# Attention followed by a gated MLP on one core: queries of pairs two to eight held in another order, and one bias row picked sooner

## The chip, the cores and the metric

The kernel runs on one core of a Trainium2 chip. The metric is the device time of one execution in microseconds (us), the median of several executions. Before the change it is 356.12 us (three runs, 356.06 to 356.26). The engines are named as in the profile: PE is TensorE (matmul), PEld its weight load, DVE VectorE, ACT ScalarE, POOL GpSimd, SP SyncE, which here only issues transfers.

## What is computed

There are 8 batches of 8 heads, 576 positions, head size 64. With q, k, v of shape (8, 8, 576, 64) and a gate s of shape (8, 8, 576):

```python
scores = (q @ k.T) / sqrt(64)
cum = cumsum(maximum(s, 0.0), axis=-1)
bias = -(cum[:, :, :, None] - cum[:, :, None, :])
scores = where(causal, -1e9, scores + minimum(bias, 0.0))
attn = softmax(scores)
x = (attn @ v) with the 8 heads of a position side by side   # (4608, 512)
h = x @ w_in                                                # (4608, 2048)
out = (h * clip(h + 3, 0, 6) / 6) @ w_out                   # (4608, 512)
```

Since cum only grows, the minimum changes nothing below the diagonal, and the bias is a difference of two numbers, one for the query and one for the key. The order of the queries within a head is free as long as bias, mask and output follow it: each query's row is computed by itself. The order of the keys is not touched by this change.

## The kernel before

**Pairs and rounds.** The 64 heads go in 32 pairs (two heads of one batch, four pairs to a batch, `PPB`). The main loop has one round per pair `p`. A round computes the scores of pair p (transposed: keys on partitions, queries along the free dimension), their exponentials into `P`, and the products with v (`av`), and prepares the queries and keys of pair p + 1. From round 4 on, pieces of the MLP (`m1`: x @ w_in with the gate, `m2`: the product with w_out) are set between the pieces of attention by `group()`, in the order of a list written out by hand (`plan`). So the order of each engine's instructions is fixed when the kernel is built.

**Queries and keys.** Pairs 0 to 10 (`NPE` = 11) come from DRAM as f16 tokens `tok` on 96 partitions (`load_qk`, line 116; GpSimd issues the transfer): each partition holds six successive positions of a head. TensorE transposes them, six transposes per operand, into a PSUM tile `pt` (`transpose_in`, line 242). A transpose takes two positions side by side, so positions of one parity come out on partitions 0 to 63 and the others on 64 to 127. Two copies (`transpose_out`, line 259; `head_out`, line 273, for one head) then bring each half down to partitions 0 to 63 of `qk`, and put the positions in order: a copy reads three columns with a stride of 96 and writes with a step of two elements. Both query copies are VectorE's; of the key copies, the first half is ScalarE's and the second VectorE's. Later pairs are transposed by the DMA's crossbar (line 286).

**Bias.** `cum` is split in parts and held in `rows_of`, tile row 1 for keys and tile row 0 for queries. For pairs 1 and up the rows are carried by a transfer (`load_aug`, line 151) to four extra rows, 64 to 67, of `qk`, so that the score matmul has 68 rows and adds the bias itself. For pair 0 there is no time for that transfer: its bias is added by a second set of matmuls (`by_rows`, lines 302 and 347) whose query side is `picked`, made by `pick(g)` (line 712) for head 1.

**Mask.** For pairs 0 to 7 (`NPROD` = 8) a matmul of `ident2` with the mask `shut` (lines 318 and 374) puts a large negative number in the upper triangles of the diagonal blocks before the scores are added. Later pairs mask on other engines.

**Output of attention.** `norm` (lines 434 and 435) divides by the sum and leaves `x` with queries on partitions. For pairs up to 6, and for pair 11, TensorE transposes x against the identity (`transpose_x`, line 449) and VectorE copies the result to `xT` (line 454); for the rest the DMA's crossbar does it (`crossbar_x`, line 462). `xT` is what `m1` reads.

**PSUM.** The eight banks go by tags. `s_bank` gives score banks from two tags of two buffers in the first four rounds, then from one tag of two. Transposes take theirs from `t_bank`: the tag "t", which has a single buffer, or, for key transposes and for `ptx` of transpose_x, the tag "po" with two buffers. "po" is open to them only while no piece of `m2` has been placed; `m2` accumulates there afterwards:

```python
def t_bank(other, name):
    if not done[2] and other:
        return psum.tile([128, 640], F16, tag="po", bufs=2, name=name)
    return psum.tile([128, 640], F16, tag="t", name=name)
```

A tile can be written once every reader of the tile that held its buffer before is done; the writing engine waits on a semaphore for that[...].

**Start.** Before round 0 the prologue makes `cum`, transposes and copies pair 0, and picks the bias row of its second head (`pick(1)`), in that order on VectorE.

Of the kernel before, what the change touches and what calls it, by code (L numbers as in the profile page):

```python
# [18 lines left out]
def kernel(  # L19
# [69 lines left out]
    w_in_sb = keep("w_in_sb", [128, NKC, DFF], F16)  # L89
    w_out_sb = keep("w_out_sb", [128, NFT, DM], F16)  # L90
    ident = keep("ident", [128, 128], F16)
    shut = keep("shut", [128, 640], F16)
    ident2 = keep("ident2", [128, 128], F16)
    stair_sb = keep("stair_sb", [128, 2, 128], F16)
    bias3 = keep("bias3", [128, 1], F32)
    rows_of = keep("rows_of", [128, 2, 640], F16, 2)
    sel = keep("sel", [128, 4], F32)
    picked = w_out_sb.rearrange("p f j -> p (f j)")[:, 0 : 2 * NROW * SEQ].rearrange(
        "p (g t) -> p g t", t=SEQ
# [9 lines left out]
    def load_qk(p, i):  # L109
        b, h0 = p // PPB, 2 * (p % PPB)  # L110
        src = (q, k)[i][b, h0 : h0 + 2]
        if not flat(p):
            if not i:
                tok = work.tile([128, 24 * D], F16, tag="tok", bufs=4, name="tok")
                toks[p] = tok[0:96].rearrange("p (i h e d) -> p i h e d", i=2, h=2, e=6)
            nc.gpsimd.dma_start(
                out=toks[p][:, i].rearrange("p h e d -> p h (e d)"),
                in_=src.rearrange("h (p e) d -> p h (e d)", e=6),
            )
        else:  # L120
            if p < NSW:
                if not i:
                    tok = work.tile([128, 24 * D], F16, tag="tok", bufs=4, name="tok")
                    toks[p] = tok[:, 0 : 18 * D]
                to, eng = toks[p], nc.gpsimd
            else:
                to, eng = raws[p % NRAW], nc.sync
            eng.dma_start(
                out=to.rearrange("p (i t d) -> p i t d", i=2, t=9)[:, i],
                in_=src.rearrange("h s d -> (h s) d").rearrange(  # L130
                    "(t p) d -> p t d", p=128
                ),
            )
# [14 lines left out]
    def load_aug(p, eng):  # L148
        for hh in range(2):
            g = 2 * p + hh  # L150
            eng.dma_start(  # L151
                out=qks[p % NQK][64:68, hh, :, 64 * hh : 64 * hh + SEQ],
                in_=rows_of[g // 32].rearrange("(r g) i t -> g r i t", g=32)[
                    g % 32, :, :, 0:SEQ
                ],
            )

# [71 lines left out]
    def transpose_in(p, i):  # L229
        tok = toks[p]  # L230
        pt = t_bank(i == 1 and p != NPROD, "pt")
        if flat(p):
            for c in range(5):
                c0 = 512 * i + 128 * c
                nc.tensor.transpose(
                    pt[:, 128 * c : 128 * (c + 1)], tok[:, c0 : c0 + 128], ident
                )
            return pt
        for hh in range(2):
            for c in range(3):  # L240
                n = 96 * (3 * hh + c)
                nc.tensor.transpose(  # L242
                    pt[:, n : n + 96],
                    tok[:, i, hh, 2 * c : 2 * c + 2, :].rearrange("p e d -> p (e d)"),
                    ident[0:96, 0:96],
                )
        return pt

    def transpose_out(
        p, i, pt, copies=(nc.vector.tensor_copy, nc.vector.tensor_copy), pars=(0, 1)  # L250
    ):
        qk = qks[p % NQK]
        if flat(p):
            order(qk, i, pt.rearrange("p (t c) -> p t c", c=128), i, copies)
            return
        copies = (nc.scalar.copy if i else copies[0], copies[1])
        for par in pars:
            to = qk[0:64, 0, i, par : par + SEQ]
            copies[par](  # L259
                out=bass.AP(  # L260
                    to.tensor,
                    to.offset,
                    [list(to.ap[0]), [2 * SPAD + 64, 2], [6, 96], [2, 3]],
                ),
                in_=pt[64 * par : 64 * par + 64, 0:SEQ].rearrange(
                    "p (h c t) -> p h t c", h=2, c=3
                ),
            )

    def head_out(p, i, hh, pt, copies):  # L270
        to = qks[p % NQK][0:64, hh, i, 64 * hh : 64 * hh + SEQ]
        for par in range(2):
            copies[par](
                out=bass.AP(
                    to.tensor, to.offset + par, [list(to.ap[0]), [6, 96], [2, 3]]
                ),
                in_=pt[64 * par : 64 * par + 64, 288 * hh : 288 * hh + 288].rearrange(
                    "p (c t) -> p t c", c=3
                ),
            )  # L280
# [20 lines left out]
    def by_rows(p, hh, out, keys, queries, stop=False):  # L301
        mm(
            out,
            lhsT=rows_of[0][:, 1, keys],
            rhs=picked[:, 2 * p + hh, queries],
            start=False,
            stop=stop,
        )

    def scores(p, hh, g):  # L310
# [4 lines left out]
        if g == 0:  # L315
            rows = slice(0, 68 if by_product else 128)
            if by_product:
                mm(S, lhsT=ident2, rhs=shut[:, 0:512], start=True, stop=False)  # L318
            for j in range(4):
                c = slice(128 * j, 128 * (j + 1))  # L320
                mm(  # L321
# [10 lines left out]
        else:  # L332
# [10 lines left out]
            if p < NROW:  # L343
                for j in ((0, 3) if g == 1 else (1, 2)):
                    c = OFF[j] - 512 * g
                    w = 448 - 128 * j
                    mm(
                        S[:, c : c + w],
                        lhsT=rows_of[0][:, 1, 128 * j : 128 * (j + 1)],
                        rhs=picked[:, 2 * p + hh, 128 * (j + 1) : SEQ],  # L350
                        start=False,
                        stop=(c != 0),
                    )
# [15 lines left out]
    def corner(p):  # L369
# [2 lines left out]
        rows = slice(0, 68 if by_product else 128)  # L372
        if by_product:
            mm(
                S.rearrange("p h c -> p (h c)"),
                lhsT=ident2,
                rhs=shut[:, 512:640],
                start=True,
                stop=False,
            )  # L380
# [63 lines left out]
    def transpose_x(p):  # L444
# [3 lines left out]
        for t in range(5):  # L448
            nc.tensor.transpose(  # L449
                pt[:, 128 * t : 128 * (t + 1)],  # L450
                x[:, t].rearrange("p h d -> p (h d)"),
                ident,
            )
        nc.vector.tensor_copy(
            out=xT[:, hp, b * SEQ : (b + 1) * SEQ], in_=pt[:, 0:SEQ]
# [129 lines left out]
    C = {}  # L585
# [19 lines left out]
    )  # L605
    for i in range(2):
        load_qk(0, i)
    fill(nc.gpsimd, shut, 0.0)
    for c in (slice(0, 512), slice(512, 640)):
        w = 128 if c.start == 0 else 64  # L610
        part = shut[:, c].rearrange("p (t c) -> p t c", c=w)
        nc.gpsimd.affine_select(
            out=part,
            in_=part,
            pattern=[[0, (c.stop - c.start) // w], [1, w]],
            compare_op=ALU.is_ge,
            fill=-65504.0,
            base=0,
            channel_multiplier=-1,
        )  # L620

    def set_stair(i, copy, heads=(0, 1)):
        for hh in heads:
# [19 lines left out]
    for i in range(NVA):  # L643
        init_va(i, nc.vector)
    nc.vector.memset(bias3, 3.0)
    fill(nc.gpsimd, rows_of[0][:, 0, :], 1.0)
    fill(nc.gpsimd, rows_of[0][:, 1, SEQ:640], 0.0)
    fill(nc.gpsimd, qks[0][64:68, 1, :, :], 0.0)
    for i in range(2):
        load_qk(1, i)  # L650
    for i in range(NQK):
        for hh in range(2):
            r = SEQ + 64 * hh
# [30 lines left out]
        )  # L684

    def cum3(n, copy, cols):
        copy(out=rows_of[n][:, 1, cols], in_=C["c"][:, cols])

    def cum4(n, eng, cols):
        eng.tensor_tensor(  # L690
            out=C["r"][64:128, cols],
            in0=C["c"][64:128, cols],
            in1=rows_of[n][64:128, 1, cols],
            op=ALU.subtract,
        )

    def cum5(n, copy, cols):
        copy(out=rows_of[n][64:128, 1, cols], in_=C["r"][64:128, cols])

    def cum6(n, eng, cols):  # L700
        lo = rows_of[n][96:128, 1, cols]
        eng.tensor_tensor(out=lo, in0=C["r"][96:128, cols], in1=lo, op=ALU.subtract)

    def new_sum():
# [3 lines left out]
    def new_rest():  # L708
        C["r"] = work.tile([128, SEQ], F32, tag="s_all", bufs=1, name="r1")

    def pick(g):
        nc.vector.tensor_scalar(
            out=picked[:, g, :],
            in0=rows_of[0][:, 0, 0:SEQ],
            scalar1=sel[:, g : g + 1],
            scalar2=None,
            op0=ALU.mult,
# [16 lines left out]
    cum3(0, A, HALVES[0])  # L734
    pick_first(HALVES[0])
    cum3(0, A, HALVES[1])
    fill(nc.gpsimd, rows_of[0][0:32, 1, 0:SEQ], -1.0)
    for i in range(2):
        load_qk(2, i)
    new_rest()  # L740
# [3 lines left out]
    for c in HALVES:  # L744
        cum6(0, V, c)
    pick_first(HALVES[1])
    nc.gpsimd.tensor_copy(out=rows_of[0][0:32, 0, 0:SEQ], in_=C["c"][0:32])
    pts = [transpose_in(0, 0)]
    head_out(0, 0, 0, pts[0], (A, A))
    warm(NWARM[1])  # L750
    pts.append(transpose_in(0, 1))
    head_out(0, 1, 0, pts[1], (V.tensor_copy, V.tensor_copy))
    head_out(0, 0, 1, pts[0], (A, V.tensor_copy))
    head_out(0, 1, 1, pts[1], (V.tensor_copy, V.tensor_copy))
    warm(NWARM[2])
    for g in range(1, 2 * NROW):
        pick(g)
    load_aug(1, nc.gpsimd)
    load_v(1, nc.sync)
    load_aug(2, nc.sync)  # L760
# [12 lines left out]
    for p in range(NP):  # L773
# [68 lines left out]
            nc.sync.dma_start(out=stair_sb, in_=stair_dram.ap())  # L842
        if p == 10:
            load_s(1, (nc.sync,) * 4)
            fill(nc.gpsimd, rows_of[1][:, 0, :], 1.0)

        if p == NPROD + 1:
            x_done[0] = NPROD
# [81 lines left out]
        scores(p, 1, 1)  # L930
        if p != PPB:
            av(p, 0, 0)
        if PPB < p < NPROD:
            transpose_x(p - 1)
        elif p >= NPROD and p != 3 * PPB:
            crossbar_x(p - 1)
        group()
        scores(p, 1, 2)
# [1 line left out]
        if p == 9:  # L940
            load_aug(11, nc.gpsimd)
        elif p == 12:
            nc.scalar.copy(out=rows_of[1][0:32, 0, 0:SEQ], in_=C["c"][0:32])
            cum3(1, nc.scalar.copy, whole)
            fill(nc.gpsimd, rows_of[1][0:32, 1, 0:SEQ], -1.0)
        av(p, 0, 1)
        norm(p, 0)
        group()
# [41 lines left out]
```

The softmax here doesn't subtract the row's maximum and nothing guards it: scores larger than these inputs give would overflow.

## Time and profile before

| what | us |
|---|---|
| time, median of three runs | 356.12 |
| span of the profiled run | 354.5 |
| TensorE busy in it | 345.6 (97%) |
| VectorE busy | 231.5 (65%) |
| ScalarE busy | 225.4 (64%) |
| GpSimd busy | 169.6 (48%) |
| VectorE query and key copies, line 259 (30 of 64x576) | 24.0, 806 ns each |
| ScalarE key copies, line 259 (10 of 64x576) | 798 ns median |
| VectorE copy of ptx to xT, line 454 (9 of 128x576) | 451 ns median |
| mean DMA rate | 136 GB/s |

The page gives busy times over the whole span, which is an average over stages with different limits. What a change in one stage is worth has to be read in that stage: the rounds 0 to 4 lie between about 10 and 34 us, rounds 5 to 8 between about 35 and 65 us, and the MLP fills TensorE from there to the end.

### The profile page before, as it was taken

To read this page: it belongs to the slowest core of one execution; us is meant where nothing else is said; L and a number is where in the kernel's file an instruction comes from. 1 tells how busy PE (TensorE), PEld (TensorE's weight loads), DVE (VectorE), ACT (ScalarE), POOL (GpSimd) and SP (SyncE) were. 2 spreads that over 40 slices of the span, in tenths; PEclk is the share of its full clock that TensorE was granted. 3 is DMA by queue.
4 is the path that set the end of the run, shared out by engine and by line. 5 is a ranking of instruction groups with operands and counts; after the bars stand their busy time and mean duration, and the time that the engine had idled before them with its cause. 6 is when DMAs were issued, how large, how long until landed. Compare 5 with 4: busy or idle time off the path is not lost.

```text
span 354.5 us, 7771 instructions
## 1 busy us (share of the span) xinstructions
PE 345.6 (97%) x2926; PEld 191.5 (54%) x2926; DVE 231.5 (65%) x472; ACT 225.4 (64%) x397; POOL 169.6 (48%) x295
## 2 busy tenths in 40 slices
PE   7889999999999999999999999999999999999995
PEld 3676666655555555555555555555555444444442
DVE  7898897677878677666666665757654553544531
ACT  6897896787787666667766666666664344433310
POOL 8987799666779556555555555555310000000000
PEclk9999999999999999999999999999999999999999
DMA  9999999999999999998788969997120100101111
GB/s 164 156 219 209 186 184 175 104 187 183 146 126 140 190 219 187 160 214 178 174 176 189 179 162 187 175 176 164 39 75 12 59 31 31 59 2 59 59 58 63
DMA packets 144438, 48.35 MB, mean 136 GB/s; under 512 B 130696, under 2 KB 139432, under 8 KB 144400
## 3 DMA queue, kind: packets, MB, share of 16 engines
q1 hardware_dynamic: 117088, 37.52, 53.4%
q0 software_dynamic: 27072, 10.05, 25.4%
q8 instruction: 23, 0.38, 0.5%
q10 hardware_dynamic: 240, 0.28, 0.2%
q14 instruction: 15, 0.12, 0.1%
HBM read 37.36 MB, written 9.44 MB: 132 GB/s over the span
## 4 chain that ended last, share of the span: by engine, by line
PE 90%; DVE 4%; ACT 3%; issue 1%; DMA 1%; ACTq 0%
PE po L505 34%; PE ph L478 34%; PE O L412 8%; PE S L336 7%; PE S L321 4%; DVE qk L259 1%; PE pt L242 1%; ACT P L355 1%; PE ptx L449 1%; DMA s_all<-in_s_dram 1%; DVE x L435 1%; PE S L318 1%; ACT tr L493 1%; DVE qk L219 1%; PE Sc L385 0%
## 5 line engine op out<-in xcount | busy, mean ns | idle before, releaser
L494 DVE SCALAR_TENSOR_TENSOR gT<-tr,ph 128x512 f16<-128x512 f32 x144 | 98.9, 687 | 97.4 <-ACT tr L493 96.3
L478 PE MATMUL ph<-xT,w_in_sb 128*128 128x512 f16 x576 | 148.1, 379 | 0.0
L505 PE MATMUL po<-w_out_sb,gT 128*128 128x512 f16 x576 | 145.8, 379 | 0.0
L493 ACT ACTIVATE tr<-ph,bias 128x512 f32<-128x512 f32 x144 | 99.1, 688 | 73.0 <-PE ph L478 70.6
L355 ACT ACTIVATE P<-S 128x512 f16<-128x512 f32 x192 | 111.4, 596 | 37.4 <-PE S L321 22.2
L478 PEld LDWEIGHTS <-w_in_sb 128*128 128x128 f16 x576 | 51.6, 97 | 44.2
L505 PEld LDWEIGHTS <-gT 128*128 128x128 f16 x576 | 50.2, 97 | 46.4 <-issue 0.2
L359 POOL TENSOR_SCALAR_AFFINE_SELECT P<-P 128x512 f16<-128x512 f16 x48 | 31.2, 650 | 45.2 <-ACT P L355 45.1
L336 PE MATMUL S<-qk 68*128 68x448 f16 (+3 forms) x256 | 49.0, 272 | 0.3 <-ACT P L355 0.2
L412 PE MATMUL O<-va,P 128*128 128x65 f16 x896 | 47.9, 193 | 0.3 <-ACT P L355 0.3
L412 PEld LDWEIGHTS <-P 128*128 128x128 f16 x896 | 39.3, 97 | 14.0 <-ACT P L355 0.5
L219 DVE COPY qk<-jt 64x768 f16<-64x768 f16 x84 | 36.6, 437 | 1.2
L336 PEld LDWEIGHTS <-qk 68*128 68x128 f16 x256 | 23.7, 98 | 24.2 <-issue 0.7
L151 POOL DMA_DIRECT2D qk<-rows_of x58 | 34.1, 591 | 2.8 <-PE S L336 1.6
L435 DVE TENSOR_TENSOR x<-O,rl 128x320 f16<-128x320 f32 x64 | 31.5, 492 | 2.2
L521 DVE TENSOR_SCALAR ob<-po 128x512 f32<-128x512 f32 (+1 forms) x36 | 24.4, 676 | 8.3 <-PE po L505 7.6
L259 DVE COPY qk<-pt 64x576 f16<-64x576 f16 x30 | 24.0, 805 | 6.4 <-ACT qk L259 5.3
L359 POOL TENSOR_SCALAR_AFFINE_SELECT PC<-PC 128x128 f16<-128x128 f16 x24 | 7.1, 294 | 41.0 <-ACT PC L393 40.9
L321 PEld LDWEIGHTS <-qk 128*128 128x128 f16 (+1 forms) x256 | 18.9, 98 | 12.7 <-DVE qk L259 0.8
L321 PE MATMUL S<-qk 128*128 128x128 f16 (+1 forms) x256 | 24.8, 219 | 0.0
L195 POOL CAST va<-vraw 128x512 f16<-128x512 f32 x32 | 21.2, 664 | 3.4 <-DMA vraw<-in_v_dram 3.3
L191 POOL CAST tok<-raw 128x576 f16<-128x576 f32 x28 | 18.1, 681 | 0.0
(71 smaller groups left out, 197.4 us busy)
## 6 DMA issues: line engine op xcount, KB each, us to landing
out_dram<-ob SPq DMA_DIRECT2D x35, 256.0 KB, 2.2
vraw<-in_v_dram SPq DMA_DIRECT2D x64, 128.0 KB, 3.8
raw<-in_q_dram SPq DMA_DIRECT2D x14, 288.0 KB, 3.7
raw<-in_k_dram SPq DMA_DIRECT2D x14, 288.0 KB
tok<-in_q_dram POOLq DMA_DIRECT2D x18, 144.0 KB, 4.9
tok<-in_k_dram POOLq DMA_DIRECT2D x18, 144.0 KB, 6.0
w_in_sb<-in_moe_w_in_dram POOLq DMA_DIRECT2D x4, 512.0 KB, 8.7
w_out_sb<-in_moe_w_out_dram POOLq DMA_DIRECT2D x8, 256.0 KB, 7.4
```

The costliest lines, as they stand in the source:

```text
L151: eng.dma_start(out=qks[p % NQK][64:68, hh, :, 64 * hh : 64 * hh + SEQ], in_=rows_of[g // 32].rearrange("(r g) i t -> g r i t", g=32)[g % ...
L219: copies[par](out=qk[0:64, :, i, 128 * par : 128 * par + 256 * n].rearrange("p h (s two c) -> p h s two c", two=2, c=128)[:, :, :, 0, :], ...
L321: mm(S[:, c], lhsT=kT[rows, c], rhs=qT[rows, c], start=(j == 0 and not by_product), stop=(j == 3 and p >= NROW),)
L336: mm(S[:, c : c + w], lhsT=kT[0:68, 128 * j : 128 * (j + 1)], rhs=qT[0:68, 128 * (j + 1) : SEQ], start=(c == 0), stop=(c != 0 and p >= NROW),)
L355: nc.scalar.activation(out=pt[:, c], in_=S, func=AF.Exp, scale=0.125)
L359: nc.gpsimd.affine_select(out=part, in_=part, pattern=[[0, part.shape[1]], [1, w]], compare_op=ALU.is_ge, fill=0.0, base=0, channel_multip ...
L412: mm(o[:, i, :], lhsT=lhsT, rhs=va[:, hh, j, 0:65], **kw)
L435: nc.vector.tensor_tensor(out=X[p][:, :, hh, :], in0=o[:, :, 0:64], in1=rl.to_broadcast([128, 5, 64]), op=ALU.mult,)
L478: mm(ph, lhsT=w_in_sb[:, kc, ft * 128 : (ft + 1) * 128], rhs=xT[:, kc, n * 512 : (n + 1) * 512], start=(kc == 0), stop=(kc == NKC - 1),)
L493: nc.scalar.activation(out=tr, in_=ph, func=AF.Relu, bias=bias3[:, 0:1])
L494: nc.vector.scalar_tensor_tensor(out=gTs[n][:, ft, :], in0=tr, scalar=6.0, in1=ph, op0=ALU.min, op1=ALU.mult)
L505: mm(po, lhsT=gTs[n][:, ft, t4 * 128 : (t4 + 1) * 128], rhs=w_out_sb[:, ft, :], start=(ft == 0), stop=(ft == NFT - 1),)
```

## The change

Three things are changed.

1. **Another order of the queries, for pairs 1 to 7** (`mixed(p, i)`: only i = 0, the queries). `load_qk` now puts four successive positions on a partition in place of six (three rows of 96 partitions cover both heads). Within each group of 64 positions, the queries then stand in the order (position mod 4, position div 4) in place of their own. In this order the two parities come out of the transposes in runs of 16 adjacent columns, and the two copies to `qk` read and write runs of 16 adjacent elements. Everything that meets the queries follows: the bias rows (a third row in `rows_of`, made by one more GpSimd copy), the mask (`shutm` beside `shut`, both now 128 columns read by broadcast), and the output: `transpose_x` takes a permutation matrix `perm` where it took the identity, which restores the order. [...]the output of pair 7 moves from `crossbar_x` to `transpose_x`, in round 8.
2. **The key copies of even pairs** (2, 4, 6) are shared otherwise: ScalarE copies the first parity of one head only, VectorE that of the other head, and then the second parity of both as before.
3. **`pick(1)` sooner**: in the prologue it goes ahead of the copies of pair 0's second head.

The diff, cut to its core:

```diff
-    shut = keep("shut", [128, 640], F16)
+    shut, shutm = keep("shut", [128, 128], F16, 2)
+    perm = keep("perm", [128, 128], F16)
-    rows_of = keep("rows_of", [128, 2, 640], F16, 2)
+    rows_of = keep("rows_of", [128, 3, 640], F16, 2)
...
+            if mixed(p, i):
+                nc.gpsimd.dma_start(
+                    out=toks[p][:, i]
+                    .rearrange("p h e d -> p (h e d)")
+                    .rearrange("p (t x) -> p t x", t=3),
+                    in_=src.rearrange("h s d -> (h s) d").rearrange(
+                        "(t p e) d -> p t (e d)", p=96, e=4
+                    ),
+                )
+                return
...
+    def mixed(p, i):
+        return i == 0 and NROW <= p < NPROD
...
     def transpose_out(
...
-        copies = (nc.scalar.copy if i else copies[0], copies[1])
+        if i and (p % 2 or p >= NPROD):
+            copies = (nc.scalar.copy, copies[1])
+        elif i:
+            head_out(p, i, 1, pt, (nc.scalar.copy,), (0,))
+            head_out(p, i, 0, pt, (nc.vector.tensor_copy,), (0,))
+            pars = (1,)
         for par in pars:
+            if mixed(p, i):
+                to = qk[0:64, 0, i, 16 * par : 16 * par + SEQ]
+                copies[par](
+                    out=bass.AP(
+                        to.tensor,
+                        to.offset,
+                        [list(to.ap[0]), [2 * SPAD + 64, 2], [32, 18], [1, 16]],
+                    ),
+                    in_=pt[64 * par : 64 * par + 64, 0:SEQ].rearrange(
+                        "p (h g v) -> p h g v", h=2, v=16
+                    ),
+                )
+                continue
...
-                ident,
+                perm if mixed(p, 0) else ident,
...
+    nc.gpsimd.tensor_copy(
+        out=mix(rows_of[0][0:32, 0, 0:SEQ]), in_=unmix(C["c"][0:32])
+    )
     pts = [transpose_in(0, 0)]
     head_out(0, 0, 0, pts[0], (A, A))
     warm(NWARM[1])
     pts.append(transpose_in(0, 1))
     head_out(0, 1, 0, pts[1], (V.tensor_copy, V.tensor_copy))
+    for g in range(1, 2 * NROW):
+        pick(g, V)
     head_out(0, 0, 1, pts[0], (A, V.tensor_copy))
     head_out(0, 1, 1, pts[1], (V.tensor_copy, V.tensor_copy))
     warm(NWARM[2])
-    for g in range(1, 2 * NROW):
-        pick(g)
...
-        if PPB < p < NPROD:
+        if PPB < p <= NPROD:
             transpose_x(p - 1)
-        elif p >= NPROD and p != 3 * PPB:
+        elif p > NPROD and p != 3 * PPB:
             crossbar_x(p - 1)
```

## The prediction

> **What bounds the kernel now.** I read the page's 40 slices first, then the waits, then the timeline of each engine where TensorE has gaps, then the same three engines at round 8, where a transpose is added. On the page:
>
> ```profile
> PE   7889999999999999999999999999999999999995
> ...
> PE 90%; DVE 4%; ACT 3%; issue 1%; DMA 1%; ACTq 0%
> ```
>
> TensorE ("PE") is short of work only in the first four slices (to about 35 us). The busy time by stage says it sharper (columns: stage, length, then PE, its weight loads, VectorE, ScalarE, GpSimd):
>
> ```profile
> 15.00:20.00 5.00, 4.61 (x91) 3.78 (x89) 4.63 (x10) 4.58 (x10) 4.47 (x9) 1.00 1.25 212
> 20.00:25.00 5.00, 4.55 (x88) 3.64 (x85) 4.81 (x10) 4.58 (x11) 4.07 (x8) 1.00 1.25 223
> ...
> 35.00:62.00 27.00, 27.00 (x308) 17.35 (x305) 23.19 (x44) 22.19 (x43) 23.77 (x33) 1.00 1.19 183
> ...
> 75.00:340.00 265.00, 264.88 (x2065) 141.94 (x2064) 168.31 (x335) 164.24 (x283) 107.54 (x191) 1.00 0.73 128
> ```
>
> From 35 us on TensorE never rests, and after 34 us its whole list of waits is one of 0.2 us. So there are two regimes. Before about 34 us a saving on another engine starts the full stretch sooner, and all of it reaches the end. After 34 us a saving on another engine is worth nothing, and anything that holds TensorE is lost in full.
>
> What bounds the first regime is VectorE. One round (a pair of heads) in its timeline:
>
> ```profile
> 18.63 0.46 DVE L454 COPY xT<-ptx 128x576 f16<-128x576 f16 x1
> 19.01 0.18 DVE L434 RECIPROCAL rl<-O 128x5 f32<-128x5 f32 x1
> 19.23 0.49 DVE L435 TENSOR_TENSOR x<-O,rl 128x320 f16<-128x320 f32 x1
> 19.64 1.63 DVE L259 COPY qk<-pt 64x576 f16<-64x576 f16 x2
> 21.30 0.20 DVE L434 RECIPROCAL rl<-O 128x5 f32<-128x5 f32 x1
> 21.53 0.49 DVE L435 TENSOR_TENSOR x<-O,rl 128x320 f16<-128x320 f32 x1
> 22.05 0.81 DVE L259 COPY qk<-pt 64x576 f16<-64x576 f16 x1
> 22.89 0.46 DVE L454 COPY xT<-ptx 128x576 f16<-128x576 f16 x1
> ```
>
> No gap: the period is 22.89 - 18.63 = 4.26 us, of which the three strided copies of L259 take 2.44. The next pair's scores start as its last key copy ends (L321 at 18.66, 22.92, 27.19). ScalarE is close behind: it starts its exponentials at 19.15 and 23.41 and idles 0.42 us between, so it needs 3.84. TensorE's issue intervals in a round add up to about 3.6.
>
> **What the skill says.** "VectorE: DVE Perf Modes", "Mode 2×_1P" and "Why PSUM operands drop a tier": a 16-bit copy with unit step handles two elements a cycle, and a PSUM source allows no more than that. The errata table of that page prices PSUM to SBUF at 120 cycles + elements/speed-up: 425 ns (estimate) for 576 elements at two, 725 at one. The trace has both kinds: xT from PSUM, contiguous, 451 ns; L259, step 2, 806 ns. "PSUM — Partial Sum Buffer", "Engine vs sequencer instructions": matmuls start and complete in program order. The trace agrees (at 11.05 to 11.93 everything behind one waiting matmul waited). So a transpose whose bank is not free holds all of TensorE.
>
> **The change, part by part.**
>
> *Query copies of pairs 1 to 7.* The innermost run becomes 16 adjacent elements on both sides in place of step 2. Bounds: 451 ns (the xT row) and 806 ns (nothing gained). I take 451: the step condition is met, and 16-element rows lose no pair. Saving 0.355 each, 0.71 a round; VectorE 4.26 - 0.71 = 3.55.
>
> *Key copies of even pairs.* ScalarE's 806 ns copy becomes a half of 480 ns (the row of L273, 64x288), and VectorE gets the other half, + 0.48. Even round: VectorE 4.03, ScalarE 3.84 - 0.33 = 3.51. Odd round: ScalarE's 3.84 is the longest. In odd rounds ScalarE's key copy now also waits for the second query copy of VectorE; queued behind it are the next three exponentials. In rounds 1 to 3 those copies end at about the time ScalarE arrives, 0 to 0.1 us.
>
> Rounds 1 to 3 load pairs 2, 3, 4: 4.03 + 3.84 + 4.03 = 11.90, against 27.19 - 14.47 = 12.72. Saving 0.8; following each wait through the three rounds by hand I get 0.9.
>
> *Pick before the copies.* Corner scores of pair 0 wait for it:
>
> ```profile
> 11.08 0.20 PE L385 MATMUL Sc<-qk 68*128 68x64 f16 x1
> 11.93 0.19 PE L302 MATMUL Sc<-w_out_sb,rows_of 128*128 128x64 f16 x1 [0.65 <-DVE w_out_sb L712]
> ```
>
> VectorE idles 9.30 to 9.77 (waiting for ScalarE's copy), and the row it multiplies is ready at 9.13, at about 9.2 with one more fill on GpSimd. So the pick (0.57 us) runs at 9.3 and pushes the next transposes 0.1 us, and the 0.65 wait goes. The gain is cut by the next chain: query copies of pair 1 end at 12.23, ScalarE's key copy 12.27 to 13.08, VectorE's 13.1 to 13.9, L321 at 13.96 in place of 14.47: 0.5.
>
> *GpSimd and DMA.* GpSimd gains a fill (0.36) and a second row copy (0.68 like L747, up to twice that if the step of 4 costs), and loses a little on the masks. The bias load of pair 1 is issued about 0.8 us later, at 10.2, and lands after 2.8 us at 13.0 (second head 13.6) against a need at 13.96: hidden, with under 1 us of slack. The query loads have 288 pieces in place of 192; the tokens of pair 1 land at about 9.3 and 10.0 against uses at 10.4 and 11.2, later ones with 3 us or more in hand. Nothing for both, up to 0.5 at worst.
>
> So TensorE enters its full stretch 0.5 + 0.9 = 1.4 us sooner (0.4 to 2.4).
>
> *Pair 7's output goes through TensorE.* The crossbar can't reorder, so round 8 gets five transposes (0.28 us for five in the chain of waits), placed behind the first matmuls of O in the second half of the round. Their output takes the PSUM tag "t", which has one bank by then (the second tag serves only until the second product has begun, at about 55 us), and the last holder is the key transpose of pair 9. It is read by ScalarE, then by VectorE:
>
> ```profile
> 61.92 1.26 ACT L624 COPY qk<-stair_sb 64x1280 f16<-64x1280 f16 x1
> 63.20 0.60 ACT L355 ACTIVATE P<-S 128x512 f16<-128x512 f32 x1
> 63.70 0.79 ACT L259 COPY qk<-pt 64x576 f16<-64x576 f16 x1
> ```
>
> ```profile
> 64.52 0.81 DVE L259 COPY qk<-pt 64x576 f16<-64x576 f16 x1 [2.91 <-ACT qk L259]
> ```
>
> ```profile
> 62.99 0.32 PE L412 MATMUL O<-va,P 128*128 128x65 f16 x5
> 63.14 1.02 PE L505 MATMUL po<-w_out_sb,gT 128*128 128x512 f16 x4
> ```
>
> The transposes stand where L505 starts at 63.14. The bank is free at 65.33. TensorE, in order, stands still for 65.36 - 63.14 = 2.2 us; queued behind are the second product, the last scores of the round and everything after. ScalarE's chain starts from TensorE's own corner matmul (61.4) and runs over the 1.26 us stair copy, so both shift together and the distance stays. Bounds: 1.9 to 2.4 by where the transposes exactly fall. With the five transposes 2.5 us, in the full regime, never given back. VectorE's added xT copy (0.45) lies in its idle time there.
>
> Masks read by broadcast and the permutation in place of the identity have the same shapes: nothing.
>
> **Sum:** 356.12 - 1.4 + 2.5 = 357.2.
>
> **Rivals.**
> - *The wait in round 8 does not bite* (the bank comes free earlier than I read, or ScalarE runs ahead). For it: the same transposes in rounds 5 to 7 wait for nothing. Against: those had two tags. 356.12 - 1.4 + 0.3 = 355.0, faster.
> - *The rounds fall to TensorE's own 3.6.* Then 12.72 - 10.8 = 1.9, + 0.5 = 2.4: 356.12 - 2.4 + 2.5 = 356.2, no change. Against: the odd rounds keep ScalarE's 3.84.
> - *Rows of 16 do not run in pairs.* Copies stay near 0.8; even pairs cost VectorE 0.48 twice and ScalarE's new wait bites by up to 0.5, which eats the pick's gain: 356.12 + 0.2 + 2.5 = 358.8. Against: the xT row and the page's condition.
>
> **Chances.** Forecast 0.57, first rival 0.16, second 0.15, third 0.12. The forecast's own spread, gains of 0.8 to 1.9 and a loss of 2.2 to 2.7, is 356.4 to 358.0. The range goes to 355.8 below, which takes in the second rival and leaves out the first, and to 358.6 above, short of the third only at its edge. Faster by over 0.2% (below 355.4): the first rival and a little, 0.17. Within 0.2% (to 356.8): the second and the lower part of the forecast, 0.22. Slower: 0.61.
>
> **What the changed profile would show.** Query copies with a shape of 64x576 at about 450 ns, right, or about 800, wrong. L321 of pairs 1 to 4 at about 14.0, 18.0, 21.8, 25.8. No wait of the corner on the pick. In round 8 a wait of TensorE's ptx on a VectorE copy of qk, about 2 us, the largest TensorE wait of the page: if it is missing, I am wrong and the kernel is faster. TensorE full from about 33 us elsewhere. I would also be wrong if the bias load of pair 1 or the first projection weights arrive late.

## The result and the profile after

| | us |
|---|---|
| before, median (356.06 to 356.26) | 356.12 |
| after, median of four executions (358.26, 358.27, 358.26, 359.91) | 358.26 |
| ratio, with its 95% interval | 1.0071 [1.0043, 1.01] |
| span of the profiled execution, before and after | 354.5, 356.5 |

The kernel became slower by 2.14 us where the forecast said 1.1: the direction is right, the size is not, and the time lies outside the forecast's own spread (356.4 to 358.0). Executions of several kernels here scatter, as these four do, so a time below is a median and the lowest is given beside it where the two differ.

On the page, the slices and the chain that ended last:

```profile
PE   8899999799999999999999999999999999999995
...
PE 89%; DVE 4%; ACT 3%; POOL 2%; issue 1%; ACTq 0%; POOLq 0%
```

TensorE is now full from the third slice on, except in the eighth (62 to 71 us). By stage (the columns are those of the prediction: PE, its loads, VectorE, ScalarE, GpSimd), first two stages of the kernel before, then those of the changed kernel:

```profile
10.00:15.00 5.00, 4.35 (x66) 3.47 (x65) 4.58 (x9) 4.34 (x9) 5.00 (x11) 1.00 0.83 135
...
62.00:75.00 13.00, 12.79 (x133) 7.64 (x131) 7.18 (x13) 10.37 (x17) 8.65 (x15) 1.00 1.15 136
```

```profile
10.00:15.00 5.00, 4.00 (x59) 2.94 (x56) 3.96 (x8) 3.45 (x8) 4.70 (x10) 1.00 0.56 88
15.00:20.00 5.00, 4.86 (x88) 4.03 (x89) 4.59 (x12) 4.63 (x11) 5.00 (x10) 1.00 1.28 206
20.00:25.00 5.00, 4.96 (x98) 4.14 (x95) 4.47 (x12) 5.00 (x12) 5.00 (x9) 1.00 1.26 206
35.00:62.00 27.00, 27.00 (x308) 17.38 (x307) 22.36 (x44) 22.16 (x42) 23.89 (x33) 1.00 1.22 195
62.00:75.00 13.00, 10.73 (x113) 6.53 (x111) 6.21 (x11) 8.17 (x14) 6.76 (x14) 1.00 0.99 131
75.00:340.00 265.00, 264.88 (x2076) 142.21 (x2075) 168.57 (x336) 165.18 (x285) 109.61 (x194) 1.00 0.76 128
```

Three places differ. From 15 to 25 us TensorE is busy 9.82 us in place of 9.16: the rounds got shorter. From 10 to 15 us it is busy 4.00 in place of 4.35: the start got worse. From 62 to 75 us it is busy 10.73 in place of 12.79: a hole of 2.06 us that was not there. From 75 us on TensorE's time is the same (264.88 both times). TensorE's waits name the causes (columns: total, times, longest):

```profile
PE ptx L518 <- DVE qk L310: 2.1, 1, 2.1
...
PE pt L253 <- DVE qk L332: 1.0, 1, 1.0
```

**The rounds.** VectorE in one round of the changed kernel; line 298 is the query copy, line 310 the key copy, line 523 the copy to xT:

```profile
18.84 0.46 DVE L523 COPY xT<-ptx 128x576 f16<-128x576 f16 x1
...
19.84 0.91 DVE L298 COPY qk<-pt 64x576 f16<-64x576 f16 x2
...
21.81 0.81 DVE L310 COPY qk<-pt 64x576 f16<-64x576 f16 x1 [0.31 <-ACT qk L310]
22.65 0.46 DVE L523 COPY xT<-ptx 128x576 f16<-128x576 f16 x1
```

Two query copies take 0.91 us, 455 ns each. The period is 22.65 - 18.84 = 3.81 us in place of 4.26, and VectorE now waits 0.31 us for ScalarE. Pair 1's scores (the first matmuls of line 388) start at 14.95 us, those of pairs 2 to 4 at 18.86, 22.68 and 26.65: three rounds of 11.70 us in place of 12.72.

**The start.** GpSimd and VectorE in the prologue; line 818 is the second copy of the bias row, line 782 the pick, line 332 the copies of pair 0:

```profile
8.80 0.68 POOL L817 CAST rows_of<-c 32x576 f16<-32x576 f32 x1
9.41 1.21 POOL L818 CAST rows_of<-c 32x576 f16<-32x576 f32 x1
```

```profile
9.51 1.29 DVE L782 TENSOR_SCALAR w_out_sb<-rows_of,sel 128x576 f16<-128x576 f16 x1 [0.39 <-POOL rows_of L817]
10.72 1.48 DVE L332 COPY qk<-pt 64x288 f16<-64x288 f16 x3
12.23 0.92 DVE L298 COPY qk<-pt 64x576 f16<-64x576 f16 x2
14.08 0.81 DVE L310 COPY qk<-pt 64x576 f16<-64x576 f16 x1 [0.92 <-ACT qk L310]
```

```profile
11.25 0.42 PE L253 MATMUL pt<-ident,tok 96*128 96x96 f16 x6 [1.00 <-DVE qk L332]
```

The pick took 1.29 us, not 0.57, and ended at 10.80, just after GpSimd's second copy (10.62). The three copies of pair 0 behind it were late, and TensorE's transposes of pair 1, which need the bank that these copies read, waited 1.00 us. The wait of the corner on the pick is gone, but a longer one on the copies stands in its place. Pair 1's scores start at 14.95 us, 0.48 later than before, where 0.5 sooner was forecast (the kernel before, then the changed one):

```profile
14.47 0.39 PE L321 MATMUL S<-qk 68*128 68x128 f16 x4
```

```profile
14.95 0.40 PE L388 MATMUL S<-qk 68*128 68x128 f16 x4
```

**Round 8.** TensorE, then VectorE:

```profile
62.47 0.32 PE L481 MATMUL O<-va,P 128*128 128x65 f16 x5
64.85 0.44 PE L518 MATMUL ptx<-perm,x 128*128 128x128 f16 x5 [2.06 <-DVE qk L310]
65.13 1.03 PE L574 MATMUL po<-w_out_sb,gT 128*128 128x512 f16 x4
```

```profile
64.00 0.80 DVE L310 COPY qk<-pt 64x576 f16<-64x576 f16 x1 [2.91 <-ACT qk L310]
```

This is the forecast's stall: the transposes of pair 7 start as VectorE's key copy leaves the bank.

The sum, each term read from these rows and those of before:

| | forecast | measured |
|---|---|---|
| pair 1's scores start | -0.51 (13.96) | +0.48 (14.95 against 14.47) |
| rounds 1 to 3 | -0.9 | -1.02 (11.70 against 12.72) |
| stall of round 8 | +2.2 | +2.23 (64.85 - 62.47, against 63.14 - 62.99) |
| five transposes | +0.28 | +0.28 (65.13 - 64.85) |
| sum | +1.1 | +1.97; the spans differ by 2.0 |

One term has the wrong sign, and it is 0.99 us. The two profiled executions took 356.22 and 358.26 us, which is 2.04 apart, as their spans are; the 2.14 between the medians has the kernel before 0.1 below its profiled execution.

### The profile page after: what moved, and what is told of

It is laid out like the page before. It is cut to its first block, busy times and chain, and to the rows that moved or that the text cites. A ratio compares the mean times of both kernels' runs of the same rounds, so it can differ in the third digit from the quotient of the medians.

```text
span 356.5 us, 7789 instructions
## 1 busy us (share of the span) xinstructions
PE 346.1 (97%) x2931; PEld 192.0 (54%) x2931; DVE 228.8 (64%) x476; ACT 224.6 (63%) x397; POOL 171.2 (48%) x299
## 4 chain that ended last, share of the span: by engine, by line
PE 89%; DVE 4%; ACT 3%; POOL 2%; issue 1%; ACTq 0%; POOLq 0%
PE po L574 34%; PE ph L547 34%; PE O L481 7%; PE S L403 7%; PE S L388 4%; ACT P L422 1%; DVE qk L310 1%; DVE x L504 1%; PE ptx L518 1%; PE pt L266 1%; PE Sc L454 1%; ACT tr L562 1%; POOL tok L127 1%; PE S L377 1%; DVE qk L230 1%
## 5 line engine op out<-in xcount | busy, mean ns | idle before, releaser
L310 DVE COPY qk<-pt 64x576 f16<-64x576 f16 x16 | 12.9, 803 | 7.3 <-ACT qk L310 7.2
```

## The experiments

Theory: VectorE's pick is held up by GpSimd's second row copy and holds up pair 1 (1 us lost); the wait for the bank in round 8 costs 2.2 us; the rounds' gain is real. Rivals: the start is late for another reason (transfers, the pick's place); the transposes themselves, not their bank, cost in round 8. Each kernel below is the changed one with the edit shown, if not said otherwise.

### The pick back in its old place

```diff
-    for g in range(1, 2 * NROW):
-        pick(g, V)
     head_out(0, 0, 1, pts[0], (A, V.tensor_copy))
     head_out(0, 1, 1, pts[1], (V.tensor_copy, V.tensor_copy))
+    for g in range(1, 2 * NROW):
+        pick(g, V)
```

> The changed kernel with the pick of pair 0's second head back in its former place, behind the four copies; all else as changed. Theory (the pick runs beside the second GpSimd row copy, is stretched from 0.57 to 1.29 us by it, and pushes the copies that free the transpose bank): the pick takes about 0.6 us at about 11.2, the first transposes of pair 1 start at about 10.3 in place of 11.25, scores of pair 1 about 0.5 us sooner, and the time falls by 0.5 us to about 357.8. Rival (the pick is slow in itself, since its source row now lies in a tile of three rows): it takes 1.3 us in the late place too, and the time is 358.3 or more.

Measured: lowest 357.55 us, median 359.39 of six. VectorE, then TensorE's waits:

```profile
11.09 0.37 DVE L782 TENSOR_SCALAR w_out_sb<-rows_of,sel 128x576 f16<-128x576 f16 x1
```

```profile
PE ptx L518 <- DVE qk L310: 2.1, 1, 2.1
...
PE Sc L361 <- DVE w_out_sb L782: 0.4, 1, 0.4
```

GpSimd's copy runs from 9.42 to 10.65 here too, but the pick comes at 11.09, when it is over, and takes 0.37 us. Pair 1's scores start at 14.21 us, 0.74 sooner than in the changed kernel; the lowest time is 0.71 below its 358.26. So the move of the pick, meant as a gain, was a loss beside that copy. Four of the six executions took 359.4 to 359.5, at a mean granted TensorE clock of 0.995 where the other two (357.55 and 357.63) show 1.0; what happens in such an execution is seen below, under the row copy on ScalarE.

### Pair 7 in its own order, through the crossbar

The output of pair 7 can then go back to `crossbar_x`, which, as it is written in both kernels, has no place for `perm`. The first two lines give pair 7 its former bias row.

```diff
-                    g % 32, :, slice(0, 3, 2) if p < NPROD else slice(1, 3), 0:SEQ
+                    g % 32, :, slice(0, 3, 2) if mixed(p, 0) else slice(1, 3), 0:SEQ
...
-        return i == 0 and NROW <= p < NPROD
+        return i == 0 and NROW <= p < NPROD - 1
...
-        if PPB < p <= NPROD:
+        if PPB < p < NPROD:
             transpose_x(p - 1)
-        elif p > NPROD and p != 3 * PPB:
+        elif p >= NPROD and p != 3 * PPB:
             crossbar_x(p - 1)
```

> The changed kernel with pair 7 left in the old order, so that its output goes by the crossbar again; pairs 1 to 6 as changed. Theory (round 8 loses 2.06 us to the wait for the transpose bank and 0.28 us to five transposes, all on TensorE's full stretch): 358.26 - 2.3 = 355.9, and no TensorE wait over 0.5 us after 35 us. Rival (what TensorE waits for there is the way of ScalarE, and shows up at the next wait for it): half or less of it comes back, 357.1 or more.

Measured: 355.75 us, ten of 13 executions from 355.71 to 355.83, ratio to before 0.9997 [0.9989, 1.0005]. The wait of ptx is gone, and 2.5 us with it, the forecast's 2.2 + 0.28. The expectation had no TensorE wait over 0.5 us after 35 us; the profiled execution, one of the three slower ones (356.76), has one of 0.74 us, on GpSimd, that comes up again below:

```profile
65.17 0.20 PE L481 MATMUL O<-va,PC 128*128 128x65 f16 x1 [0.74 <-POOL PC L426]
```

### The same transposes in another bank

```diff
-        pt = t_bank(True, "ptx")
+        if p == NPROD - 1:
+            pt = psum.tile([128, 640], F16, tag="ph", bufs=2, name="ptx")
+        else:
+            pt = t_bank(True, "ptx")
```

> The changed kernel with the five transposes of pair 7 kept, but written to a bank of the MLP's first product, which is idle in round 8. Theory (it is the bank, not the transposes, that costs): 358.26 - 2.1 = 356.2, that is 0.3 above the kernel that leaves the five transposes out. Rival (the transposes themselves, or the weights they load, hold TensorE): 357.5 or more.

Measured: 356.09 us (11 of 13 from 356.07 to 356.10). TensorE's list of waits has no ptx. All five transposes and the permutation are still there, so it is the bank that cost 2.17 us; against the crossbar the transposes cost 356.09 - 355.75 = 0.34, near the 0.28 of the sum.

### The kernel before, with the pick sooner and nothing else

```diff
     head_out(0, 1, 0, pts[1], (V.tensor_copy, V.tensor_copy))
+    for g in range(1, 2 * NROW):
+        pick(g)
     head_out(0, 0, 1, pts[0], (A, V.tensor_copy))
     head_out(0, 1, 1, pts[1], (V.tensor_copy, V.tensor_copy))
     warm(NWARM[2])
-    for g in range(1, 2 * NROW):
-        pick(g)
```

> The kernel before with the sooner pick alone; no second row copy on GpSimd. Theory (the place is good, the neighbour is bad): the pick runs at about 9.3 in 0.57 us, the corner no longer waits 0.65 us, scores of pair 1 start 0.3 to 0.5 us sooner, 355.6 to 355.8. Rival (the sooner place itself is bad, since the copies behind it hold the transpose bank): 356.1 to 356.5.

Measured: 355.51 us (355.28 to 355.71, 21 executions), ratio 0.9983 [0.9976, 0.9989]: faster by 0.61.

```profile
9.32 0.37 DVE L712 TENSOR_SCALAR w_out_sb<-rows_of,sel 128x576 f16<-128x576 f16 x1
9.76 1.51 DVE L273 COPY qk<-pt 64x288 f16<-64x288 f16 x3
```

Here GpSimd has no copy at that moment (it starts none between 9.13 and 10.60), the pick runs in VectorE's gap as the forecast had it, and pair 1's scores start at 13.84 us (14.47 before). The idea was right; its neighbour in the changed kernel undid it.

### The same, with one useless copy on GpSimd

To separate that neighbour from all else of the change: the kernel above with the second row copy alone, into a tile that nobody reads.

```diff
+    spare = keep("spare", [128, 640], F16)
...
     nc.gpsimd.tensor_copy(out=rows_of[0][0:32, 0, 0:SEQ], in_=C["c"][0:32])
+    nc.gpsimd.tensor_copy(
+        out=spare[0:32, 0:SEQ].rearrange("p (g w v) -> p g w v", w=4, v=16),
+        in_=C["c"][0:32].rearrange("p (g v w) -> p g w v", w=4, v=16),
+    )
```

> The kernel before with only the pick sooner, and one more GpSimd copy just after the bias row's: 32x576, f32 to f16, read with a step of four, into a tile that nobody reads (the changed kernel's second row copy, without anything that uses it). Theory (that copy alone makes the pick slow, by sharing something with VectorE): the pick takes about 1.3 us in place of 0.37, and the time is 355.51 plus 0.5 to 0.9, about 356.2. Rival (the pick of the changed kernel is slow because of its transfers or its other reader): the pick takes 0.4 to 0.6 us, and the time is 355.5 to 355.7.

Measured: 356.41 us (356.21 to 356.52, 13 executions). GpSimd, then VectorE:

```profile
9.03 1.24 POOL L749 CAST spare<-c 32x576 f16<-32x576 f32 x1
```

```profile
9.30 1.45 DVE L713 TENSOR_SCALAR w_out_sb<-rows_of,sel 128x576 f16<-128x576 f16 x1
10.68 1.50 DVE L274 COPY qk<-pt 64x288 f16<-64x288 f16 x3
```

The pick is 0.37 us without the copy and 1.45 with it, though neither reads or writes what the other writes. Pair 1's scores start at 14.75 us, 0.91 later than without, and the time is 0.90 longer. GpSimd's queue behind the copy is later too, so its transfers start later; but from 10 to 35 us none of TensorE's waits in this trace is on a transfer, while the one of 0.81 us at 11.20 is on VectorE's copies behind the pick. This one copy accounts for nearly all of the term that was 0.99 us off, and it shows the failed step by itself.

### The key copies of even pairs shared as before

```diff
-        if i and (p % 2 or p >= NPROD):
+        if i:
             copies = (nc.scalar.copy, copies[1])
```

> The changed kernel, with the key copies of even pairs shared as before the change: ScalarE copies the first parity of both heads. Theory (ScalarE's 3.84 us sets such a round, since VectorE then needs only 4.26 - 0.71 = 3.55): the rounds that load pairs 2 and 4 take about 3.84 us in place of 3.91 and 3.97, so the score matmuls of pairs 1 to 4 span about 11.5 in place of 11.70 us and the time is about 358.1. Rival (the split is needed, because ScalarE's whole key copy waits behind VectorE's second query copy): those two rounds grow by about 0.3 us each, to 4.2, and the time is about 358.9.

Measured: lowest 358.27 us, median 359.12 of six, the lowest equal to the changed kernel's 358.26. Pairs 1 to 4 start at 14.95, 18.70, 22.52 and 26.52: 11.57 us in place of 11.70, so ScalarE's whole copy does fit, as the theory had it, and the rival's 4.2 us rounds do not come. But pair 5's scores start at 31.53 against 31.52: round 4 gives the 0.13 back. In these two profiles the new sharing of key copies is worth nothing, either way. Which wait of round 4 took the 0.13 stays open.

### The second row copy on ScalarE

```diff
-    nc.gpsimd.tensor_copy(
-        out=mix(rows_of[0][0:32, 0, 0:SEQ]), in_=unmix(C["c"][0:32])
-    )
...
     head_out(0, 0, 1, pts[0], (A, V.tensor_copy))
+    A(out=mix(rows_of[0][0:32, 0, 0:SEQ]), in_=unmix(C["c"][0:32]))
```

> The changed kernel, with the second copy of the bias row (reordered queries) made by ScalarE after its copies of pair 0, not by GpSimd beside VectorE's pick. Theory (the GpSimd copy lengthens the pick from 0.4 to 1.29 us): the pick takes 0.37 to 0.57 us, the first transposes of pair 1 start about 10.4 in place of 11.25, score matmuls of pair 1 start at about 14.0 to 14.4 in place of 14.95, and the time is about 357.5. The wait of round 8 stays, 2.1 us. Rival (the pick is slow or late for another reason, or the bias load of pair 1, issued later now, becomes the wait): no gain, 358.0 to 358.5.

Measured: lowest 357.57 us, median 358.67 of six. VectorE:

```profile
9.51 0.37 DVE L782 TENSOR_SCALAR w_out_sb<-rows_of,sel 128x576 f16<-128x576 f16 x1 [0.39 <-POOL rows_of L817]
```

The pick is as early as in the changed kernel and takes 0.37 us. Pair 1's scores start at 14.22, 0.73 sooner, and the lowest time is 0.69 below. That is the theory's number in the lowest execution. The profiled execution took 359.32, and it shows what the others lose. TensorE before and at round 8, then two stages (the third figure from the end is the granted TensorE clock):

```profile
61.27 0.59 PE L574 MATMUL po<-w_out_sb,gT 128*128 128x512 f16 x2 [0.54 <-DMA w_out_sb<-in_moe_w_out_dram]
...
64.28 0.69 PE L518 MATMUL ptx<-perm,x 128*128 128x128 f16 x5 [1.56 <-DVE qk L310]
64.76 1.91 PE L574 MATMUL po<-w_out_sb,gT 128*128 128x512 f16 x4
```

```profile
64.00:66.00 2.00, 1.72 (x8) 0.94 (x8) 0.68 (x2) 0.00 (x0) 1.95 (x6) 0.57 1.84 122
66.00:68.00 2.00, 2.00 (x17) 1.25 (x15) 0.28 (x2) 0.60 (x1) 2.00 (x4) 0.58 0.44 37
```

After two standstills, of 0.54 us and then of 1.56 us with 1.4 us of work between them, TensorE ran at about half clock: four 128x512 matmuls took 1.91 us, against 1.03 in the changed kernel's profile. In stretches of half a microsecond the granted clock is 0.50 from 64.5 to 67.5, with 0.77 before and 0.82 after, which adds up to 3.4 us at half clock. That is 3.4 / 2 / 357.6 = 0.5% of the span, and the mean clock of this execution is 0.995.

The mean clock is on record for every execution, traced or not. Four kernels keep the stall (this one, the changed one and those with the pick late and without the split). Of their 22 executions 11 lie 1.65 to 1.95 us above the lowest of their kernel, and just these 11 show 0.992 to 0.995; the other 11 show 0.997 to 1.0. Of the 113 executions of the nine kernels without the stall, three are as low (two of those with the other bank, 357.34 and 357.37, and one of 359.56 further below). So with the stall about half of the executions meet the half clock, and without it hardly any. Why only half of them do is open.

### Both losses taken out, in two ways

The first has the pick back in its old place and pair 7 through the crossbar; the second has the row copy on ScalarE and pair 7 through the crossbar (the edits are those shown above).

> The changed kernel, with both suspected losses taken out: the pick where it was before the change, and pair 7 in its own order with its output through the DMA's crossbar. Theory (the two losses are independent, and both carry in full to the end): 357.55 - 2.5 = 355.05, about 355.1. Rival (one loss only uncovers another limit, such as GpSimd's late masks): not below 355.7, what the crossbar alone gave.

> The changed kernel, with the second row copy on ScalarE (the pick stays sooner) and pair 7 in its own order through the crossbar. Theory (all gains and no loss: 0.6 from the pick as measured alone, 1.0 from the rounds): 356.12 - 1.6 = 354.5, and at most 354.9. Rival (ScalarE's added copy delays its key copy of pair 1 by its own 0.6 to 0.8 us): 355.3 or above.

Measured: the first 355.61 us (lowest 355.06, highest 357.66, 14 executions, ratio 0.999 [0.9978, 1.0002]); the second 355.65 (355.05 to 358.09, 14 executions, 0.9994 [0.9981, 1.0007]). The lowest of the first, 355.06, is the theory's 355.05; most executions are above it, and neither median beats 355.51, the pick alone. The second missed its 354.9 in every execution. Part of the reason is in its start: ScalarE's row copy (1.22 us from 9.37) puts its first exponentials back to 10.50 and its key copy of pair 1 to 12.34, against 10.01 and 11.84 with the pick alone, half a microsecond where the rival named 0.6 to 0.8. So pair 1's scores start at 14.18 us, not at the 13.84 of the pick alone, and hardly sooner than with the pick late (14.21). The other part is in round 8 (GpSimd, then TensorE; an execution of 356.47):

```profile
64.36 0.28 POOL L426 TENSOR_SCALAR_AFFINE_SELECT PC<-PC 128x128 f16<-128x128 f16 x1
```

```profile
64.70 0.20 PE L481 MATMUL O<-va,PC 128*128 128x65 f16 x1 [0.74 <-POOL PC L426]
```

The same mask and the matmul that needs it, in the kernel before:

```profile
62.16 0.29 POOL L359 TENSOR_SCALAR_AFFINE_SELECT PC<-PC 128x128 f16<-128x128 f16 x1
```

```profile
64.51 0.19 PE L412 MATMUL O<-va,PC 128*128 128x65 f16 x1
```

There GpSimd was done at 62.45, 2.06 us ahead of the use. Here TensorE would come to it at 63.96, 0.55 sooner, and GpSimd comes 2.20 us later. So it is mostly GpSimd's own lateness that costs the 0.74. In both kernels GpSimd waits over 3 us for a load of v, but here its cast of that v starts at 39.97 us, and at 37.19 in the kernel before; from 40 to 65 us it hardly rests (24.5 of 25 us busy) and makes little of it up. The first kernel's trace (357.31) has two such waits, of 0.88 and 0.74 us. So GpSimd's mask is the next limit here, and it is one where GpSimd is late.

### GpSimd relieved at VectorE's expense, with a control

In rounds 5 to 7 GpSimd makes two stair copies each (`set_stair`: a constant pattern, `stair_sb`, that goes into `qk` for a later pair, one copy for each head). One of the two goes to VectorE; first in the kernel with the row copy on ScalarE and the crossbar, then in the kernel before with the pick sooner.

```diff
-                set_stair((p + 3) % NQK, nc.gpsimd.tensor_copy)
+                set_stair((p + 3) % NQK, nc.gpsimd.tensor_copy, (0,))
+                set_stair((p + 3) % NQK, nc.vector.tensor_copy, (1,))
```

> The kernel with ScalarE's row copy and pair 7 through the crossbar, and in rounds 5 to 7 the stair copy of one of the two heads on VectorE in place of GpSimd (1.25 us off GpSimd in each). Theory (in the kernel without this edit GpSimd reaches its mask of PC in round 8 at 64.36 us, 0.74 us after TensorE needs it, so part of the gain of the rounds is given back there): the wait of TensorE on GpSimd's mask is gone and the time is 354.9 to 355.1 in nearly all executions. Rival (late loads, not GpSimd's work, hold the middle of the kernel): GpSimd just waits longer for loads, the time stays 355.5 to 355.7 and as spread as before, 355.1 to 358.

> Control: the kernel before with only the pick sooner, and the same stair copies on VectorE. Theory (there GpSimd's masks are not late, TensorE is full from 35 us): 355.5, as without the stair edit. Rival (GpSimd or the stair copies limit that kernel too): 355.2 or less; or VectorE's added copies delay the next pair's keys: 355.8 or more.

Measured: 356.9 us (356.45 to 359.56, 15 executions) and 357.76 (357.46 to 358.51, five): both worse by over a microsecond than without the edit. In the first the wait on the mask did go (GpSimd waited 0.48 us for ScalarE there and wrote it at 62.66), but the time was lost before: TensorE waited 0.8 us for gT, which VectorE writes, and 0.4 for a key copy of VectorE; in the control it waited 2.5 us for gT. I had not expected VectorE to be short of time there. The control's GpSimd and VectorE in round 6:

```profile
44.07 1.25 POOL L624 COPY qk<-stair_sb 64x1280 f16<-64x1280 f16 x1
```

```profile
44.13 1.53 DVE L624 COPY qk<-stair_sb 64x1280 f16<-64x1280 f16 x1
```

The same VectorE copy takes 0.49 us in the control's rounds 5 and 7. Here it lasts until 0.34 us after GpSimd's copy ended: the pick's story again, in another place.

### GpSimd relieved at nobody's expense

From the second kernel with both losses out, the bias loads of pairs 8 and 9 go to SyncE's queue, behind its loads of v:

```diff
-            elif p in (6, 7):
-                load_aug(p + 2, nc.gpsimd)
...
             load_v(p + 2, nc.sync)
+        if p in (6, 7):
+            load_aug(p + 2, nc.sync)
```

> The kernel with ScalarE's row copy and pair 7 through the crossbar, and in rounds 6 and 7 the bias loads of pairs 8 and 9 issued by SyncE, behind its loads of v, in place of GpSimd (1.2 us off GpSimd in each of the two; VectorE gets nothing). Theory (GpSimd's late arrival at the mask of round 8 costs TensorE 0.7 us there): GpSimd reaches the mask of PC about 2.4 us sooner, at about 62, TensorE doesn't wait for it, and the time is 355.0 to 355.1. Rival (what is gained there is lost at the next wait, for late loads of w_out or v): 355.5 to 355.7 and as spread as without the edit.

Measured: 354.76 us (354.41 to 355.08, five executions), ratio 0.9964 [0.995, 0.9977]: below the kernel before, the changed one, and the pick alone. GpSimd:

```profile
60.77 0.29 POOL L426 TENSOR_SCALAR_AFFINE_SELECT PC<-PC 128x128 f16<-128x128 f16 x1 [1.14 <-ACT PC L462]
```

Now GpSimd waits for ScalarE and not TensorE for GpSimd; after 34 us TensorE waits only 0.2 us in all, as in the kernel before. But not all of the 0.9 us against the kernel without the edit can be put down to the edit, for two reasons. Its cast of v, which started at 39.97 us there, starts at 36.34 here, ahead of any edited instruction; those 3.6 us are more than the 0.74 by which the mask was late. And the end of the program is shorter here: the last VectorE copy ends at 349.95 us (351.00 in the kernel before, 350.30 with the pick alone), and the span ends 2.85 us after it, where that takes 3.4 to 3.6 us in the traces of all other kernels. Some 0.6 us of the profiled execution's gain lies there, behind all computation, and why is open. With an end of 3.5 us this execution would have taken about 355.1 (an estimate: 354.5 + 3.5 - 2.85), near the two higher of the five (355.06 and 355.08) and the theory's 355.0 to 355.1. That even the highest of the five is about the lowest of the other's fourteen, 355.05, speaks for the edit; five executions and one trace don't show it.

## Why the prediction was off

**Right, with size.** Query copies: 0.355 us less each was forecast, 0.806 - 0.455 = 0.351 came. Rounds 1 to 3: 0.9 forecast, 1.02 came. The wait in round 8, its cause and its place: 2.2 forecast, 2.23 came; another bank gave back 2.17, and the crossbar, which leaves out the five transposes too, 2.51. The bias load of pair 1, issued later, stayed hidden: no wait names it. The stall is lost in full, as forecast: the stages after 75 us are alike, and both ways of removing it gave all of it back. None of the three rivals happened: the stall did bite, the rounds fell to 3.9 us and not to 3.6, and rows of 16 did run in pairs.

**The step that failed** is "So the pick (0.57 us) runs at 9.3 and pushes the next transposes 0.1 us, and the 0.65 wait goes". The 0.57 was taken from a row and carried to another moment, where VectorE's neighbour was another. At 9.41 GpSimd starts the copy that the change adds, and the pick lasts 1.29 us. The transposes were pushed by a microsecond, the query copies of pair 1 ended at 13.15 where the forecast had 12.23, and the chain behind them nearly kept the forecast's distances: the gain of 0.5 became a loss of 0.48. (The row was also ready later than the 9.2 that was forecast, at 9.48; with ScalarE making the second copy this cost nothing that shows, since VectorE's next copies start at 9.79, and at 9.77 in the kernel before.) The kernel with the useless copy shows it alone: 1.45 against 0.37 us, 0.90 us of time. The addition was counted under GpSimd and DMA, with "Nothing for both", because only its data's deadline was asked after, not what it runs beside.

The Trainium skill states what I left out: "SBUF — State Buffer", "Who interferes with whom", says that VectorE's copies and tensor-scalar operations in the fast two-port modes share a pair of SBUF ports with GpSimd, that whichever instruction starts first holds the pair to its end, and that the other blocks fully. The runs agree in three places (1.29 and 1.45 us for a pick of 0.37, 1.53 for a stair copy of 0.49), each ending 0.2 to 0.5 us after GpSimd's copy did. That the cause is these ports, and not something else that the two engines share, no run here separates; that it is the copy, the useless one shows. Even the 0.57 of before had it: that pick started at 11.31 beside a GpSimd copy that ended at 11.47:

```profile
11.31 0.57 DVE L712 TENSOR_SCALAR w_out_sb<-rows_of,sel 128x576 f16<-128x576 f16 x1
```

```profile
11.16 0.31 POOL L196 CAST va<-vraw 64x128 f16<-64x128 f32 x1
```

**A premise too wide.** "A saving on another engine ... all of it reaches the end" held for the 0.5 us of the changed kernel's sum, and for the 0.6 of the pick alone. With the losses taken out (1.0 us and more was to be gained) it did not hold in most executions: GpSimd's mask in round 8 takes a part when GpSimd is late. And "a saving on another engine is worth nothing" after 34 us must not be turned round: work added to VectorE there cost 1.25 us (356.9 - 355.65) and, in the control, 2.25 us (357.76 - 355.51).

**Not settled.** Why v lands earlier in some executions than in others; what makes the half clock come in one execution and not in the next; how much of the last kernel's gain is its edit's, and why its end is shorter.

## What to carry to other kernels

When an instruction is moved, ask what runs on the neighbouring engine at the new moment, and take its duration from a row with the same neighbour: here a VectorE copy within SBUF that started beside a GpSimd copy lasted until that copy had ended, 1.29 us in place of 0.37. When a transpose or any matmul takes a bank from a tag with one buffer, find the last reader of that bank and read its time from the trace: TensorE stood still until then, 2.06 us here. And before a gain is said to reach the end, read on each other engine how far ahead of TensorE it is at the next meeting, and ask whether the change makes that engine later: GpSimd was 2.06 us ahead at the mask, more than the gain, and was late all the same, because it came 2.20 us later itself.

## What was new about the hardware

- A VectorE instruction of 0.37 us from SBUF to SBUF took 1.29 to 1.45 us beside a GpSimd copy of 1.2 us that shares no data with it. GpSimd's copy itself was no longer for it (1.21 and 1.24 us; 1.23 where the pick came later).
- GpSimd's row copy took 0.68 us reading in order and 1.21 with a step of four elements; ScalarE took 1.22 for the latter.
- VectorE's copy from PSUM took 455 ns for 64x576 f16 in rows of 16 elements on both sides, the same as for one unbroken row (451).
- Standstills of 0.54 and 1.56 us, 1.4 us apart, were followed, in the traced execution, by 3.4 us at half of TensorE's clock (0.50 in each half microsecond from 64.5 to 67.5 us). The Trainium skill, "TensorE: Matmul & The Clock Gate", "What's actually happening", speaks of an idle window of about 3.4 us that runs free; here 2.1 us of idle time in 3.6 us were enough, in some executions and not in others (the changed kernel's profile, with a gap of 2.06 us, kept the full clock). An execution that has met it can be told without a trace: its mean granted clock is 0.992 to 0.995.
